# Planning steps 28 to 31 of the first pair with the rest, loading the weights in another order, and a subtraction moved to another engine

## The chip, the cores and the metric

The kernel runs on one core of a Trainium2 chip. The metric is the device time of one execution in microseconds (us), as the median of several runs. The engines are named as in the profile: PE (matmul; PEld is its weight load), DVE (vector), ACT (scalar), POOL (GpSimd) and SP, which here issues nearly all DMAs. Each engine works through its own queue in order. An instruction that waits for a semaphore holds up everything behind it on that engine.

## The reference

```python
B, H, S, Ns, D = (8, 8, 512, 32, 64)      # x: (B,H,S,D), state: (B,H,Ns,D)
scores = scale * np.matmul(x, state.transpose(0, 1, 3, 2))
a = softmax(scores);  xread = np.matmul(a, state)
scores2 = scale * np.matmul(state, x.transpose(0, 1, 3, 2))
a2 = softmax(scores2); sread = np.matmul(a2, x)
attn_out = np.concatenate([xread, sread], axis=2)
x = attn_out.transpose(0, 2, 1, 3).reshape(B * (S + Ns), H * D)   # 4352 x 512
h = x @ w_in                                # 512 x 2048
g = h * np.cos(h)
return g @ w_out                            # 2048 x 512
```

(`softmax` stands for the reference's maximum, subtraction, exponential and division.)

## The kernel before

**Tiles and steps.** A batch has 512 tokens. A tile is 128 of the 2,048 hidden columns by the 512 tokens of a batch, so a batch has 16 tiles (NF) and a pair of batches 32 (PERIOD). Step n of the program belongs to tile n. Since `xread` is a product with the small `state`, the kernel multiplies `state` with `w_in` ahead of time (`products`, kept in `sw_all`), and a tile is then one product of depth 256 with the attention weights `aT_all`: `hidden` (line 476). A tile's cosine gate follows on two engines in turn: `gate` (ACT, 547), `gate2` (DVE, 550), `gate3` (ACT, 553) and `gate4` (DVE, 567), which writes g into a slot of `g_all` and frees the tile's PSUM bank for the next tile but one. In the first pair two banks are used for single tiles; from the third batch on, tiles go in twos and by seven products of half size in place of eight (`seven_part`, `seven_sum`, `sw_sums` and `halves` make and use the sums).

**The output products.** g @ w_out is made for two batches together, as a 2 by 2 block product, again by seven block products in place of eight. Two of its blocks in the first pair are plain: `first_product` (weights a11, quad 5) and `second_product` (weights a12, quad 6), eight PE parts each (621). The others (p5, p3, p6 and so on, `Product`, line 750) have seven stages each, whose weights come from blocks kept in DRAM through a ring of four buffers (`fetch_block`). The operands of p5 are differences of rows of g, made by `outer_sum`, and differences of quarters of those, made on POOL by `Product.sums`. A "quad" is a piece of `g_all` of four slots of 512 elements; quads 5 to 8 hold the four quarters a11, a12, a21, a22 of w_out, others hold g, raw data and temporaries. Rows 0 to 3 of g (`quads_of[0, r]`) are tiles 0-7, 8-15, 16-23 and 24-31; row 2 lies in quads 10 and 9.

**Conversion.** The weights arrive as 64-bit floats. `fetch(i)` loads piece i raw into the quad `SLOTS[i]`, and `convert` makes 32-bit floats of it by two ACT instructions ("1", line 219, and "2", line 222, which goes to the scratch `aS_all`, named E0 to E3), two on DVE ("b", 225, and "c", 228; "c" is the last to read the raw data) and one on POOL ("d", 233). Pieces 4, 5, 7, 8, 10 and 11 are of w_in; 6 and 9 are a11, 12 and 13 are a12, 14 and 16 are a22, and 15 and 17 are a21. The sums of these quarters that p5 and the others need are made by `inner_weight` on POOL (671) and `sums_of` (1304), and are sent to DRAM by SP (`send_raw`, 659; `send_inner`, 674).

**The order.** Up to step FIRST - 1 = 27 the order on each engine comes from a list scheduler inside the program: `first_pair_tasks` lists tasks with an engine, a cost, what they read and write, and a due step (k in the calls of `at_step`); `link` turns a due step into a due time and hands it back along the dependences; `first_pair` then walks an estimated time, takes at each point the task that can start soonest on its engine, within NEAR, and among these the one with the smallest due time plus four times its delay, and issues it. From step 28 on `later_pair` and the loop below it issue in an order written out by hand: gates, `part`s of the attention, `stages(step)` of the products, `outer_at`, `sums_at`, `weights_at`, output stores (`store`, sent by SP at the start of the next step) and loads (`load_now`). The tile of a step is computed by PE two steps ahead of its gate in this part.

```python
CONV = range(4, N_LOADS)
CONV_DUE = (3, 3, 3.5, 6, 6, 7, 9, 9.5, 11, 12, 13, 14, 15, 16)
...
for step, t in enumerate(all_tiles[FIRST:], FIRST):
    ...
    later_pair(step, t, all_tiles[step + 2:step + 3])
```

Of the kernel before, what the change touches and what calls it, by code (L numbers as in the profile page):

```python
# [22 lines left out]
def kernel(  # L23
# [47 lines left out]
    quads_free = [7]  # L71
# [110 lines left out]
    def out_load(m, f):  # L182
# [11 lines left out]
    SLOTS = ((9, 9, 10, 10, 11) + (3, 2, 9, 10, 11) + (3, 9, 10, 11)  # L194
             + (9, 10, 11, 9))
# [48 lines left out]
    class Attention:  # L244
# [182 lines left out]

        def keep2(self):
            nc.tensor.transpose(out=at[1][:, 0:P],
                                in_=self.sr.rearrange("p j d -> p (j d)"),  # L430
                                identity=ident)
# [82 lines left out]
    def seven_part(t, k):  # L514
        (b11, b12, b21, b22), swS = weights_of(t)
        aT, aS = aT_of[t.b], aS_all[:, t.b % 2]
        h1, h2 = [h_pairs[t.at][:, i] for i in range(2)]
        for out_, w, r, start in (
                ((h2[:, LO], b11, aT[:, 0, LO], True),
                 (h2[:, HI], swS[:, 0], aS[:, 0], False)),  # L520
                ((h2[:, LO], swS[:, 1], aS[:, 1], False),
                 (h1[:, LO], b12, aT[:, 1, LO], False)),
                ((h2[:, LO], b21, aS[:, 2], False),
                 (h1[:, HI], swS[:, 2], aT[:, 1, HI], False)),
                ((h2[:, LO], b22, aS[:, 3], False),))[k]:
            nc.tensor.matmul(out=out_, lhsT=w, rhs=r, start=start, stop=True,  # L526
                             skip_group_check=True)
        if k == 0:
            nc.scalar.copy(h1[:, LO], h2[:, LO])
            nc.scalar.copy(sums_all[:, 0], h2[:, HI])  # L530

    def seven_sum(t, k):
# [5 lines left out]

    quads_of = defaultdict(list, {(0, 0): [0, 1], (0, 1): [2, 3],
                                  (0, 2): [10, 9], (0, 3): [5]})  # L540
# [54 lines left out]

    def store(b, half, src):

        def go(ch):
            ot = osb.tile([P, S], F32, name="ot")
            nc.vector.transpose(out=ot.rearrange("p (j i) -> p j i", i=32),  # L600
                                in_=src.t[:, ch].rearrange(
                                    "p (j i) -> p j i", i=32))
            rows = out[b * T:b * T + S, :].rearrange("(j t) d -> t j d", t=32)
            src.done()

            def send():
                for q in range(P // 32):
                    c0 = HD * half + P * ch + 32 * q
                    nc.sync.dma_start(
                        out=rows[:, :, c0:c0 + 32],  # L610
                        in_=ot[32 * q:32 * q + 32].rearrange(
                            "p (j i) -> p j i", i=32))
            stores_due.append(send)
        n = now[0] + 2 * (now[0] < PERIOD - 4)
        later.extend([(n + 1, lambda: go(0)), (n + 2, lambda: go(1))])
# [19 lines left out]
    def second_kept(pr, ch):  # L635
        if ch == 0:
            pr.o = Held()
        plus(pr.o, ch, acc[ch], pr.u)
        if ch == 1:
            store(2 * pr.n, 0, pr.o)  # L640
# [59 lines left out]
    class Product:  # L700
# [17 lines left out]
        def sums(self, k):  # L718
            lo, hi = self.quads()
            engine = nc.gpsimd  # L720
            if k == 1:
                self.q1 = quads_free.pop(0 if self.n else 1)
                self.t1 = quad(self.q1)[:, :, LO]
                self.t2 = quad(self.q1)[:, :, HI]
                sub(engine, self.t1, lo[:, :, HI], lo[:, :, LO])
            elif k == 2:
                sub(engine, self.t2, hi[:, :, HI], self.t1)
            elif k == 3:
                self.t3 = lo[:, :, HI]
                if not self.in_place:  # L730
                    self.q3 = quads_free.pop(0)
                    self.t3 = quad(self.q3)[:, :, LO]
                sub(engine, self.t3, hi[:, :, HI], lo[:, :, HI])
            else:
                sub(engine, self.t1, hi[:, :, LO], self.t2)

        def stage(self, k, copy):
            pr, b, c = self.pr, self.b, self.c
# [10 lines left out]
            for i in range(QT):  # L749
                nc.tensor.matmul(out=o, lhsT=ring[(self.first + k) % NB][:, i],  # L750
                                 rhs=g[:, i], start=(start and i == 0),
                                 stop=(i == QT - 1), skip_group_check=True)
            t5, u2 = sums_all[:, 1], sums_all[:, 2]
            if k == 1:
                copy(b[:, LO], c[:, LO])  # L755
                copy(t5, c[:, HI])
            elif k == 2:
                nc.vector.tensor_tensor(u2, c[:, LO], t5, op=ALU.add)
                self.sums(4)
            elif k == 3:  # L760
                copy(b[:, HI], u2)  # L761
            elif k == 4:
                nc.vector.tensor_tensor(c[:, HI], c[:, LO], t5, op=ALU.add)
                if not self.in_place:
                    quads_free.append(self.q3)
                if self.frees:
                    quads_free.append(quads_of[self.row][0])
            elif k == 5:
                self.out(0, b)
                if self.frees:  # L770
                    quads_free.extend(quads_of[self.row][1:])
            elif k == 6:
                self.out(1, c)
                quads_free.append(self.q1)
# [28 lines left out]
    products = []  # L803
# [260 lines left out]
    A11, A12, A21, A22, SQ = 5, 6, 7, 8, 11  # L1064
    temps = [quad(TEMPS), aS_all.rearrange("p n i s -> p (n i s)").rearrange(
        "p (t s) -> p t s", s=S)]
    for at_, freed in ((27, A22), (27, TEMPS), (28, SQ)):
        weights_at[at_].append(lambda freed=freed: quads_free.append(freed))
# [22 lines left out]
    FIRST = PERIOD - 4  # L1091
# [8 lines left out]
    def first_pair_tasks():  # L1100
# [124 lines left out]
        def attention_late(b, k):  # L1225
# [7 lines left out]
            for j in range(2):  # L1233
                add("pe", 1.05, lambda j=j: (part(b, "reads", j) if b > 1
                                   else a.reads(j)),
                    f"xT{j} {x}", "at0", k + 1 + j)
            for i in range(NK):
                add("dve", .3, lambda i=i: a.keep((i,)), "at0 i20 i21", "sr",
                    k + 2)
            if b < 2:  # L1240
                add("pe", .2, a.keep2, "sr", "at1", k + 3)
                add("act", .18, a.keep3, "at1", f"sT{b}", k + 3)

        def products(b, nt, k, c0=0, c1=WC):
# [3 lines left out]
            if nt == 0 and c1 - c0 == WC:  # L1248
# [3 lines left out]
                    for j in range(2)]  # L1252
            sw = [f"sw{nt % 2}{h}{j}" if half else
                  f"sw{nt % 2}0{j} sw{nt % 2}1{j}" for j in range(2)]
            add("pe", .55 if half else 1.05,
                lambda: attn[b].products(nt, SIDE, c0, c1), w + f" stT{b // 4}",
                " ".join(side), k)
            for j in range(2):
# [4 lines left out]
                        nt, SIDE, c0, c1,  # L1263
# [3 lines left out]
        def tile_(t, k):  # L1267
# [10 lines left out]
            add("dve", dve(512) - .02, lambda: gate4(t), f"h{h} q{h}", g)  # L1278
# [40 lines left out]
        def second(i, k):  # L1319
# [3 lines left out]
            if i == NH - 1:  # L1323
                for ch in range(2):
                    add("dve", .6, lambda ch=ch: second_kept(pr, ch),
                        "acc held0", "held1", k + 1)

        for b in (1, 2):
            attn[b] = Attention(b)
# [12 lines left out]
        for step, what in (  # L1342
# [7 lines left out]
                (5, lambda: attention(1, 6)),  # L1350
# [3 lines left out]
                (13, lambda: attention_late(1, 14)),  # L1354
# [4 lines left out]
                (16, lambda: inner(3, matrix(SQ), SQ, temps[1], E, 17)),  # L1359
                (17, lambda: sums_of(A22, SQ, A11, sub_, 18, "pool")),  # L1360
                (17, lambda: attention(2, 19)),
# [3 lines left out]
                                   names(TEMPS), 20)),  # L1365
                (20, lambda: sends(1, a12, 6, 22)),
                (21, lambda: inner(4, matrix(A22), A22, temps[1], E, 22)),
# [4 lines left out]
                (25, lambda: attention_late(2, 25)),  # L1372
                (24, lambda: [add("sp", .4, lambda n=n: fetch_block(n), "B3",
                                  f"ring{n}", 27) for n in range(NB - 1)])):
            at_step[step].append(what)
        for step, t in enumerate(all_tiles[0:FIRST]):
# [3 lines left out]
            if 4 <= step < 4 + NH:  # L1380
                first(step - 4, step - 1)
            if 13 <= step < 13 + 2 * NH and step % 2:
                second((step - 13) // 2, step)
        for i in range(2):
            o, x1, x2 = 0, 10, 0
            n = range(2 * i, 2 * i + 2)
            add("dve", dve(1024), lambda i=i: outer_sum(nc.vector, 0, 0, 2, 0,
                                                        0, i),
                names(10, *n) + " " + names(0, *n), names(0, *n), 27, True)
        return tasks  # L1390

    CONV = range(4, N_LOADS)
    CONV_DUE = (3, 3, 3.5, 6, 6, 7, 9, 9.5, 11, 12, 13, 14, 15, 16)
    PACE, NEAR, SEND = 3.6, .3, 2.5
# [37 lines left out]
    def first_pair():  # L1432
        now[0] = FIRST - 1
# [20 lines left out]
        while can:  # L1454
            best = None
            for e in free:
# [4 lines left out]
                for t in mine:  # L1461
                    at_ = max(free[e], ready[t])
                    if t.shares and pool_busy[0] <= at_ < pool_busy[1]:
# [4 lines left out]
                        key=lambda t: t.due + 4.0 * (starts[t] - soon))  # L1468
# [28 lines left out]
        for what in weights_at[FIRST - 1]:  # L1497
            what()
        for what in outer_at[FIRST - 1]:
            outer_sum(*what)  # L1500
        for pd, k in sums_at[FIRST - 1]:
            pd.sums(k)
        load_now(4)
# [52 lines left out]
    for step, t in enumerate(all_tiles[FIRST:], FIRST):  # L1556
        s, even = step % NF, step % 2 == 0
        if (s == 0 or step == FIRST) and t.b < B:
            steps = plan(t.b)
# [67 lines left out]
```

## Time and profile before

| what | value |
|---|---|
| median of 3 runs | 740.38 us (738.02 to 741.12) |
| profiled execution, its own time | 741.05 us |
| its span | 739.2 us |
| PE busy / DVE / POOL / ACT | 707.2 / 509.2 / 544.1 / 340.4 us |
| first tile's matmul | 22.24 us |
| tile 16, matmul and `gate4` | 99.26 and 103.56 us |
| tile 28, matmul | 143.00 us |
| first PE instruction of step 32 | 164.72 us |

The profile gives busy time by engine and stretch, groups of instructions by line with the idle time before them and what ended it, a chain of work followed back from the end, and the instructions in order of time. Times inside an execution are counted from the span's start. Lines L476, L621, L750 and L526 are PE's tiles, plain products, staged products and half-size tiles.

### The profile page before, as it was taken

To read this page: it belongs to the slowest core of one execution; us is meant where nothing else is said; L and a number is where in the kernel's file an instruction comes from. 1 tells how busy PE (TensorE), PEld (TensorE's weight loads), DVE (VectorE), ACT (ScalarE), POOL (GpSimd) and SP (SyncE) were. 2 spreads that over 40 slices of the span, in tenths; PEclk is the share of its full clock that TensorE was granted. 3 is DMA by queue.
4 is the path that set the end of the run, shared out by engine and by line. 5 is a ranking of instruction groups with operands and counts; after the bars stand their busy time and mean duration, and the time that the engine had idled before them with its cause. 6 is when DMAs were issued, how large, how long until landed. Compare 5 with 4: busy or idle time off the path is not lost.

```text
span 739.2 us, 10736 instructions
## 1 busy us (share of the span) xinstructions
PE 707.2 (96%) x3610; PEld 516.6 (70%) x3610; DVE 509.2 (69%) x716; ACT 340.4 (46%) x563; POOL 544.1 (74%) x528
## 2 busy tenths in 40 slices
PE   8899898699999999999999999999999999999997
PEld 3343333277778778777778788777688788888886
DVE  5989899876866668849756577768665467355550
ACT  5888867344463446344634464344634533211110
POOL 2467489587998997588998665879989665799600
PEclk9999999999999999999999999999999999999999
DMA  9984998846245954692238735752225465345661
GB/s 299 271 240 151 268 215 251 253 108 136 85 128 120 209 176 111 144 198 86 78 84 167 162 96 113 144 159 84 73 68 120 114 213 135 108 156 202 161 157 38
DMA packets 212471, 112.40 MB, mean 152 GB/s; under 512 B 158336, under 2 KB 175232, under 8 KB 212416
## 3 DMA queue, kind: packets, MB, share of 16 engines
q1 hardware_dynamic: 211328, 111.19, 57.4%
q8 instruction: 29, 0.48, 0.3%
q10 hardware_dynamic: 960, 0.39, 0.2%
q14 instruction: 26, 0.21, 0.1%
q0 software_dynamic: 128, 0.13, 0.1%
HBM read 88.08 MB, written 23.59 MB: 151 GB/s over the span
## 4 chain that ended last, share of the span: by engine, by line
PE 60%; POOL 21%; DVE 10%; issue 3%; ACT 3%; DMA 1%; SPq 0%; POOLq 0%; DVEq 0%; ACTq 0%
PE o L750 29%; POOL g_all L697 16%; PE h L526 13%; PE h L476 8%; POOL swS_all L509 3%; PE at L308 3%; PE at L851 2%; PE o L621 2%; PE at L413 2%; POOL sw_all L509 2%; DVE g_all L697 1%; DVE g_all L567 1%; DVE w_in L228 1%; DVE q_all L550 1%; PE o L851 1%
## 5 line engine op out<-in xcount | busy, mean ns | idle before, releaser
L697 POOL TENSOR_TENSOR g_all<-g_all 128x512 f32<-128x512 f32 x256 | 336.6, 1348 | 65.2 <-DVE g_all L697 48.7
L750 PE MATMUL o<-g_all 128*128 128x256 f32 x1456 | 344.1, 381 | 2.4 <-POOL g_all L697 2.4
L750 PEld LDWEIGHTS o<-g_all 128*128 128x128 f32 x1456 | 273.5, 190 | 49.7 <-issue 5.5
L550 DVE TENSOR_TENSOR q_all<-q_all,h 128x1024 f32<-128x1024 int32 (+1 forms) x88 | 85.1, 970 | 44.2 <-ACT q_all L547 43.9
L547 ACT ACTIVATE q_all<-h 128x1024 int32<-128x1024 f32 (+1 forms) x88 | 73.0, 834 | 86.3 <-PE h L526 35.1
L553 ACT ACTIVATE q_all<-q_all,halfpi 128x1024 f32<-128x1024 f32 (+1 forms) x88 | 84.0, 956 | 40.5 <-DVE q_all L550 40.2
L567 DVE TENSOR_TENSOR g_all<-h,q_all 128x1024 f32<-128x1024 f32 (+1 forms) x88 | 85.7, 974 | 19.8 <-ACT q_all L553 18.3
L535 DVE TENSOR_TENSOR h<-h,sums_all 128x256 f32<-128x256 f32 x96 | 41.2, 429 | 75.9 <-PE h L526 55.9
L476 PE MATMUL h<-aT_all,sw_all 128*128 128x512 f32 x128 | 63.6, 623 | 13.4 <-DVE g_all L567 12.5
L526 PE MATMUL h<-aT_all,sw_all 128*128 128x256 f32 x192 | 59.6, 392 | 3.8 <-DVE g_all L567 3.4
L526 PE MATMUL h<-aS_all,swS_all 128*128 128x256 f32 x192 | 60.2, 395 | 2.6 <-ACT sums_all L530 1.8
L526 PE MATMUL h<-aS_all,sw_all 128*128 128x256 f32 x192 | 58.0, 384 | 0.2
L697 DVE TENSOR_TENSOR g_all<-g_all 128x1024 f32<-128x1024 f32 x40 | 57.0, 1441 | 0.1
L476 PEld LDWEIGHTS h<-aT_all,sw_all 128*128 128x128 f32 x128 | 22.9, 191 | 45.9 <-DVE g_all L567 22.0
L526 PEld LDWEIGHTS h<-aS_all,swS_all 128*128 128x128 f32 x192 | 33.9, 189 | 27.0 <-issue 11.3
L755 ACT COPY o<-o 128x256 f32<-128x256 f32 x26 | 9.3, 357 | 85.4 <-PE o L750 85.4
L526 PEld LDWEIGHTS h<-aT_all,sw_all 128*128 128x128 f32 x192 | 34.5, 189 | 16.3 <-DVE g_all L567 12.2
L509 POOL TENSOR_TENSOR swS_all<-sw_all 128x128 f32<-128x128 f32 x48 | 22.8, 475 | 29.1 <-ACT sw_all L450 29.1
L761 ACT COPY o<-sums_all 128x256 f32<-128x256 f32 x26 | 9.8, 378 | 68.8 <-PE o L750 68.8
L526 PEld LDWEIGHTS h<-aS_all,sw_all 128*128 128x128 f32 x192 | 35.6, 190 | 8.4 <-DVE h L535 2.7
L233 POOL TENSOR_TENSOR w_in<-w_in,aS_all 128x1024 int32<-128x1024 int32 (+1 forms) x10 | 21.2, 2131 | 26.8 <-DVE w_in L228 24.9
L590 DVE SCALAR_TENSOR_TENSOR held<-o,held 128x512 f32<-128x512 f32 x40 | 27.2, 681 | 13.7 <-PE o L750 13.1
(115 smaller groups left out, 924.8 us busy)
## 6 DMA issues: line engine op xcount, KB each, us to landing
g_all<-blocks_kept SPq DMA_DIRECT2D x206, 256.0 KB, 2.8
blocks_kept<-g_all SPq DMA_DIRECT2D x48, 256.0 KB, 3.7
g_all<-in_moe_w_out_dram SPq DMA_DIRECT2D x8, 1024.0 KB, 5.7
out_dram<-ot SPq DMA_DIRECT2D x128, 64.0 KB, 2.0
g_all<-in_moe_w_in_dram SPq DMA_DIRECT2D x6, 1024.0 KB, 6.2
xT<-in_x_dram SPq DMA_DIRECT2D x96, 64.0 KB, 2.9
x_b<-in_x_dram SPq DMA_DIRECT2D x24, 256.0 KB, 4.7
x_b<-in_x_dram SPq DMA_DIRECT2D x16, 128.0 KB, 4.1
```

Of the source, the lines that this page charges most:

```text
L308: nc.tensor.matmul(out=(to or at)[j][Ns * k:Ns * k + Ns, n0:n1], lhsT=w[D * j:D * j + D, self.b, Ns * k:Ns * k + Ns], rhs=r(slice(D * j, D ...
L476: nc.tensor.matmul(out=t.hp, lhsT=t.lhs(i), rhs=t.rhs(i), start=(i == 0), stop=(i == t.kn - 1))
L509: nc.gpsimd.tensor_tensor(o, x1, x2, op=op)
L526: nc.tensor.matmul(out=out_, lhsT=w, rhs=r, start=start, stop=True, skip_group_check=True)
L535: nc.vector.tensor_tensor(o, h2[:, LO], sums_all[:, 0], op=ALU.add)
L547: nc.scalar.activation(t.q.bitcast(I32), t.hp, func=ACTF.Copy, bias=0.25)
L550: nc.vector.tensor_tensor(t.q, t.q.bitcast(I32), t.hp, op=ALU.subtract)
L553: nc.scalar.activation(t.q, t.q, func=ACTF.Sin, bias=halfpi, scale=-TWO_PI)
L567: nc.vector.tensor_tensor(g, t.hp, t.q, op=ALU.mult)
L590: nc.vector.scalar_tensor_tensor(out=out.t[:, ch], in0=bank, scalar=TWO_PI, in1=b.t[:, ch], op0=ALU.mult, op1=ALU.add)
L697: engine.tensor_tensor(o[:, i:i + n], x1[:, i:i + n], x2[:, i:i + n], op=ALU.subtract)
L750: nc.tensor.matmul(out=o, lhsT=ring[(self.first + k) % NB][:, i], rhs=g[:, i], start=(start and i == 0), stop=(i == QT - 1), skip_group_ch ...
```

## The change

The list scheduler takes tiles 0 to 31 (`FIRST = PERIOD`), and with them everything that the hand order did in steps 28 to 31: the second half of the first outer sum, five of the seven stages of p5 with their POOL sums and fetches, the loads of batch 3, the halves and weight sums of batch 2, the seven half-size products of tile 32, p3's first POOL sum and the two output stores. The conversion order puts a22 and a21 (14 to 17) ahead of a12 (12, 13), and the raw data go into quads 9, 10 and 6, no longer into 11. The second product's eight parts come at steps 16 to 27 (before 13 to 27, every other one), the first product's are due 1.5 steps later. The outer sum (2, 3, 2, 0) goes from POOL to DVE and into the planned part. Scaling `sread` by the inverse sums (`keep`, four DVE instructions of 32 rows) becomes eight ACT instructions (`keep_scaled`) for batches 1 and 2. The weight of a delay in the scheduler's choice goes from 4 to 8.

```diff
-    SLOTS = ((9, 9, 10, 10, 11) + (3, 2, 9, 10, 11) + (3, 9, 10, 11)
-             + (9, 10, 11, 9))
+    SLOTS = ((9, 9, 10, 10, 11) + (3, 2, 9, 10, 6) + (3, 9, 9, 10)
+             + (10, 6, 9, 10))
+        def keep_scaled(self, k):
+            rows = slice(Ns * k, Ns * k + Ns)
+            for j in range(2):
+                c0 = 2 * D * j + D * (k % 2)
+                nc.scalar.activation(self.sr[rows, j],
+                                     at[0][rows, c0:c0 + D], func=ACTF.Copy,
+                                     scale=self.i2[rows, j:j + 1])
-    FIRST = PERIOD - 4
+    FIRST = PERIOD
             for i in range(NK):
-                add("dve", .3, lambda i=i: a.keep((i,)), "at0 i20 i21", "sr",
-                    k + 2)
+                if b:
+                    add("act", .36, lambda i=i: a.keep_scaled(i),
+                        "at0 i20 i21", "sr", k + 2)
...
+        def outer(o, x1, x2, half, k, engine):
+            q, a_, b_ = [quads_of[0, r][half] for r in (o, x1, x2)]
+            for i in range(2):
+                n = range(2 * i, 2 * i + 2)
+                add(engine, dve(1024) if engine == "dve" else 2 * pool(512),
+                    lambda i=i: outer_sum(nc.vector if engine == "dve"
+                                          else nc.gpsimd, 0, o, x1, x2, half,
+                                          i), ...
+        def p5_tasks(k):
+            ...
+                add("pool", 4 * pool(512), lambda i=i: pd.sums(i), r, w,
+                    k - 3 + i)
...
+        t32, t34 = all_tiles[PERIOD], all_tiles[PERIOD + 2]
+                (26, lambda: outer(0, 2, 0, 0, 26, "dve")),
+                (27, lambda: outer(0, 2, 0, 1, 27, "dve")),
+                (28, lambda: tokens_of_next(30)),
+                (28, lambda: products(2, 0, 28)),
+                (28, lambda: p5_tasks(30.0)),
+                (29, lambda: weight_columns(t32, 30)),
...
+                (30, lambda: seven_tasks(t32, 30)),
+                (31, lambda: weight_columns(t34, 32)),
+                (32, lambda: outer(2, 3, 2, 0, 32, "dve")),
+                (32, lambda: p3_sums(32))):
             if 4 <= step < 4 + NH:
-                first(step - 4, step - 1)
-            if 13 <= step < 13 + 2 * NH and step % 2:
-                second((step - 13) // 2, step)
+                first(step - 4, step - -0.5)
+            for i in range(NH):
+                if SECOND_AT[i] == step:
+                    second(i, step)
-    CONV = range(4, N_LOADS)
-    CONV_DUE = (3, 3, 3.5, 6, 6, 7, 9, 9.5, 11, 12, 13, 14, 15, 16)
+    SECOND_AT = (16, 17, 19, 20, 22, 24, 26, 27)
+    CONV = (4, 5, 6, 7, 8, 9, 10, 11, 14, 15, 16, 17, 12, 13)
+    CONV_DUE = (3, 3, 3.5, 7.5, 6, 8.5, 9, 9.5, 10.5, 11, 12, 13.8, 14, 15)
-                        key=lambda t: t.due + 4.0 * (starts[t] - soon))
+                        key=lambda t: t.due + 8.0 * (starts[t] - soon))
```

The stores are made by a function `stored` that returns its four DMAs, so that the scheduler can place the DVE transposition and the sending apart; `Product.stage` is split into `multiply` and `follow` for the same reason. A few other due steps of the weights' sums and of the attention are moved by one to three steps.

## The prediction

> **What bounds the kernel.** I read the page first: PE is busy for 96% of the span, and the forty slices show where it is not, at the start, around slices 7 to 8 of the first pair, and at the end. Then I cut the time up to 200 us into stretches. The columns are PE, PEld, DVE, ACT and POOL busy, granted clock, DMA share and GB/s.
>
> ```profile
> 40.00:77.48 37.48, 32.62 (x133) 13.99 (x133) 34.15 (x39) 30.95 (x45) 25.74 (x12) 1.00 0.64 209
> 77.48:124.00 46.52, 46.28 (x197) 18.68 (x198) 42.35 (x62) 33.13 (x53) 33.12 (x21) 0.96 0.88 229
> 124.00:147.56 23.56, 15.88 (x77) 6.37 (x75) 20.35 (x28) 9.88 (x15) 15.29 (x12) 0.93 0.90 268
> 147.56:164.72 17.16, 17.16 (x75) 12.63 (x68) 12.12 (x18) 8.41 (x16) 13.97 (x17) 1.00 0.41 92
> 40.00:140.00 100.00, 90.23 (x385) 37.88 (x385) 91.75 (x120) 72.03 (x108) 71.64 (x42) 0.98 0.82 239
> 40.00:164.72 124.72, 111.94 (x472) 51.67 (x473) 108.97 (x144) 82.37 (x127) 88.11 (x60) 0.97 0.75 212
> 164.72:200.00 35.28, 34.73 (x189) 26.36 (x188) 28.49 (x36) 13.53 (x24) 30.93 (x31) 1.00 0.49 120
> ```
>
> Up to 140 us DVE is at 91.75%; PE has all its spare time here too. The bound changes hands: DVE in 40-77, PE in 77-124 (46.28 of 46.52), DVE again in 124-147, PE from 147.56 on. From step 32 (164.72) PE is at 98%, so a microsecond won before 164.72 reaches the end, and one won behind it doesn't show here. What stops PE before 165 us is one thing, the gate of an earlier tile on DVE; the columns are the total, how often, and the longest.
>
> ```profile
> PE h L476 <- DVE g_all L567: 10.8, 6, 4.5
> ```
>
> Two of these stalls are long. The instructions in order of time show them, with the wait in brackets:
>
> ```profile
> 77.48 2.61 PE L476 MATMUL h<-aT_all,sw_all 128*128 128x512 f32 x4 [3.82 <-DVE g_all L567]
> ...
> 136.54 1.98 PE L476 MATMUL h<-aT_all,sw_all 128*128 128x512 f32 x4
> 143.00 3.27 PE L476 MATMUL h<-aT_all,sw_all 128*128 128x512 f32 x4 [4.47 <-DVE g_all L567]
> ```
>
> A tile costs 1.72 us in the chain of waits elsewhere. After each long stall it costs more: 2.61 and then 2.79 for the next product, and 3.27 and then 1.36 in place of 1.02. That is 1.96 and 1.89 us. In both stretches of 5.5 us the granted clock is 0.69; after the stalls of 1.47 us and less it stays at 1.00. So PE's useful work in 40-164.72 is 111.94 - 3.85 = 108.1 us.
>
> Why tile 28 waits until 143.00 is on DVE:
>
> ```profile
> 135.37 2.04 DVE L697 TENSOR_TENSOR g_all<-g_all 128x1024 f32<-128x1024 f32 x1
> 137.34 0.87 DVE L423 TENSOR_TENSOR sr<-at,i_all 32x128 f32<-32x128 f32 x3
> 138.23 1.61 DVE L697 TENSOR_TENSOR g_all<-g_all 128x1024 f32<-128x1024 f32 x1
> 139.87 0.30 DVE L423 TENSOR_TENSOR sr<-at,i_all 32x128 f32<-32x128 f32 x1
> 140.18 0.69 DVE L590 SCALAR_TENSOR_TENSOR held<-o,held 128x512 f32<-128x512 f32 x1
> 140.79 1.27 DVE L550 TENSOR_TENSOR q_all<-q_all,h 128x512 f32<-128x512 int32 x2
> ```
>
> The outer sum and the scaling are queued ahead of the gates of tiles 26 and 27, and PE has nothing else: the eight second products were used up by 124 us.
>
> **The change part by part.** I count up to the first PE instruction of step 32, since both programs have the same work done there.
>
> DVE. Removed: 8 scalings of batches 1 and 2 (0.58 + 0.60 + 0.87 + 0.30 = 2.35 us in the rows of L423). Added: the outer sum (2, 3, 2, 0), two instructions of 128x1024; L697 on DVE took from 1.22 (148-149 us) to 2.04, on average 1.44, so 2.4 to 4.1, and I take 2 x 1.44 = 2.9. Gates, halves, transpositions and conversions stay in number. Sum: 108.97 - 2.35 + 2.9 = 109.5 us.
>
> ACT. 16 new instructions of 32x64 out of PSUM. The nearest rows are L434 (128x128 out of PSUM, 0.28) and L352 (128x2, 0.19): 3.0 to 4.5 us, nearer to L434, so 4. They lie in stretches where ACT is at 33.13 of 46.52 and 9.88 of 23.56. Without that cover a gate behind one waits 0.28 us.
>
> POOL. Removed: four instructions of 1.27 = 5.1 us at 161-171. In the whole kernel L750 waited 2.4 us for POOL, so this is worth 0 to 2.4; I take 0, because PE is full right behind it. POOL's inner sums (101.33 to 136.33 before) can begin sooner, since a21 and a22 no longer wait for a12.
>
> That last point can cost something. DVE's conversion at 72.08 took 3.27 us in place of 1.23; POOL's instruction ran from 71.58 to 74.26, and 74.26 + 1.1 is just its end. So a DVE instruction that comes behind a POOL one waits it out. POOL's share is 33.12 of 46.52 us in 77-124; an inner sum of 1.27 delays a collision by 0 to 1.27. Of the 14 conversions and two dozen other two-input instructions perhaps ten more meet one, at half of it: 6 us on DVE at worst, and 0 if as many collisions go from 101-136. I take 0, since the POOL instructions are moved and not added. The Trainium skill (SBUF — State Buffer, "Who interferes with whom") says that a DVE instruction with two SBUF inputs and a GpSimd one that reads SBUF lock each other out for the whole instruction, the first to issue winning; that speaks against bringing an outer sum to DVE next to p5's POOL sums. By the rule both new instructions would wait out a POOL one, and the sum would be the 4.1 above, 1.2 us more than mine.
>
> PE. No work is added. The second products go from steps 13-27 to 16-27 and the first ones 1.5 steps back, so 10 to 14 us of fillers leave 77-124, where PE is the bound, and lie in 124-147 and around 77, where it waits. The two clock losses (3.85 us) go if no stall of 3.8 us is left.
>
> SP. 48 block sends, the two stores (eight DMAs; 1.95 us for four at 158.35) and the loads of batch 3 are now issued in the planner's order. The transfers are used at 90% in 124-147. p5's fetches stand behind the stores; if a store waits for its transposition, a stage waits for its block: 0 to 2 us, taken as 0, since three blocks are fetched ahead.
>
> The sum. The same engine stays the bound, and the question is its share. If DVE keeps in the last 25 us the 91.75% that it has in 40-140, step 32 begins at 40 + 109.5 / 0.9175 = 159.3 and not at 164.72: 5.4 us. PE would be at 108.1 / 119.3 = 91% until then, about what it has in 40-140 (90.23), so it doesn't forbid this. The profiled execution would go from 741.05 to 735.7, the median of the runs (0.67 lower) from 740.38 to **735.0 us**.
>
> Bounds. The best 10 us slices of DVE have 96.5 to 97.4%; 96.5% throughout gives 40 + 113.5 = 153.5, a gain of 11.2 (729.2). With the whole stretch's share as it was, 108.97 / 124.72 = 87.4%, step 32 begins at 165.3: a loss of 0.6 (741.0).
>
> **The rivals.** *More than forecast* (0.10): PE's fillers and the tail both fall into place, 727 to 732. For it: PE and DVE alone need only 108 to 110 us of 124.72. Against it: they need each other, and DVE never held 96% for over 10 us at a time.
>
> *No difference* (0.17): the stalls move and DVE's share stays at 87.4%: 741. For it: the tail's DVE work (halves, transpositions, gates of four tiles) waits on PE and can't be drawn forward. The planner prices p5's sums at five us, while a sum is two POOL instructions of 1.27, so its order in the tail rests on wrong times.
>
> *Slower* (0.23): the raw quads become the wait. Before, pieces 12 to 17 went through quads 9, 10 and 11; now 14, 17 and 13 all follow piece 8 in quad 10, which tile 16's `gate4` must write next. The fetches, each right behind the last DVE "c" of its quad:
>
> ```profile
> 47.54 4.27 SPq L206 DMA_DIRECT2D g_all<-in_moe_w_out_dram  x2
> ...
> 71.50 0.37 SPq L206 DMA_DIRECT2D g_all<-in_moe_w_out_dram  x1
> ...
> 84.23 0.39 SPq L206 DMA_DIRECT2D g_all<-in_moe_w_out_dram  x1
> ```
>
> From a fetch to the end of its "c" pieces 12 to 17 took 23.9, 23.9, 19.5, 17.6, 19.9 and 12.6 us, mean 19.6. Piece 8's "c" ended at 47.48. Three turns at the mean end at 106.3; tile 16's `gate4` was at 103.56. Over (103.56 - 47.48) / 3 = 18.7 us a turn, tile 16 is later than before. At the mean it is 2.7 us late, PE has no second product yet (a12 is converted last) and pays a clock loss of 1.9: 740.38 + 4.6 = 745. Against it: the last piece needed 12.6 (8.4 of it for the DMA, by ACT's wait at 92.67), and three such turns end at 85.3; the long turns were work put off, not waiting for data. The collisions with POOL above would end in the same place, 740.38 - 5.4 + 6 = 741, or slower together with it.
>
> **How the numbers follow.** The forecast itself (732 to 736.7) has 0.50, more than forecast 0.10, no difference 0.17, slower 0.23. About 0.5% (3.7 us, 736.7 to 744.1) is what a measurement of this kernel can tell from no change. So faster 0.60, same 0.17, slower 0.23. The range reaches from the first bound with some of the POOL gain (728.5) to just over the slower case (746); cases of both signs hold much of the chance, and the forecast's own range is 732 to 736.7.
>
> **What would show it.** Right: step 32's first PE instruction at 157 to 162; stalls of PE behind L567 under 7 us in 40-165 and none over 3; L621 spread to 140 us; DVE over 90% until step 32; the rest from step 32 to the end unchanged within 1 us. Wrong: `gate4` of tile 16 later than 104 us behind an ACT or DMA wait; DVE conversions stretched over 2 us in numbers; L750 waiting for a block; or the time won before step 32 lost again behind it on POOL or DVE, which I price at nothing.

## The result and the profile after

The changed kernel takes 750.38 us (median of 4 runs, 749.98 to 751.37) against 740.75 us for the kernel before beside it; the ratio is 1.0139, with a 95% interval of 1.0110 to 1.0167. It is 10 us slower where 5 us faster was forecast. Its profiled execution has a span of 748.2 us, 9.0 more than before. Cut at two marks that both programs have, the first tile on PE and the first PE instruction of step 32, the stretches show where. First the kernel before, then the changed one (PE, PEld, DVE, ACT and POOL busy, granted clock, DMA share, GB/s):

```profile
22.24:164.72 142.48, 127.06 (x569) 58.87 (x570) 126.01 (x171) 98.18 (x149) 97.44 (x64) 0.98 0.77 217
...
164.72:739.20 574.48, 561.68 (x2968) 449.91 (x2966) 370.27 (x523) 230.90 (x397) 440.82 (x454) 1.00 0.52 130
```

```profile
33.95:173.65 139.70, 127.77 (x570) 59.43 (x570) 126.38 (x166) 98.54 (x163) 102.09 (x64) 0.98 0.73 206
...
173.65:748.20 574.55, 561.59 (x2968) 449.92 (x2966) 369.93 (x523) 231.81 (x398) 434.85 (x449) 1.00 0.53 130
```

The first tile comes at 33.95 and not at 22.24: 11.71 us lost. From there to step 32 the new order needs 139.70 in place of 142.48: 2.78 won. Behind step 32 nothing changes (0.07). Together that is the 9.0. So two things are to be explained: a stall ahead of the first tile, and a gain half as large as forecast.

The stall is on ACT. These are its instructions in order of time, before and after, around the first exponential (L348):

```profile
14.97 0.66 ACT L222 ACTIVATE aS_all<-g_all 128x512 int32<-128x512 uint32 x1
15.54 1.14 ACT L348 ACTIVATE aT_all<-aT_all 128x512 f32<-128x512 f32 x2
16.95 1.16 ACT L219 ACTIVATE w_in<-g_all 128x1024 f32<-128x1024 f32 x1 [0.28 <-DMA g_all<-in_moe_w_in_dram]
```

```profile
15.00 0.67 ACT L222 ACTIVATE aS_all<-g_all 128x512 int32<-128x512 uint32 x1
28.31 1.12 ACT L219 ACTIVATE g_all<-g_all 128x1024 f32<-128x1024 f32 x1 [12.64 <-DMA g_all<-in_moe_w_out_dram]
29.33 1.14 ACT L348 ACTIVATE aT_all<-aT_all 128x512 f32<-128x512 f32 x2
```

A conversion of a piece of w_out now stands ahead of the exponential of batch 0, and its data are not there. The exponential needs nothing of it, but ACT works in order. Behind the exponential the whole first attention waits: DVE stands still for 12.53 us until 29.98, and PE for 12.41 until its first tile. SP's queue says why the data are late:

```profile
9.15 13.87 SPq L143 DMA_DIRECT2D held<-in_state_dram  x8
23.07 0.43 SPq L206 DMA_DIRECT2D g_all<-in_moe_w_out_dram  x1
```

The eight loads of the state hold SP until 23.0 us, as they did before (9.29 to 22.9). The fetch goes out at 23.07 and lands 5.2 us later. The planner, though, starts with `"sp": 10.0`, as it did before: it believes that SP can issue at 10 us. Piece 9's raw data now go into quad 6, which nobody has used, so nothing in the plan holds its fetch back; by the planner's own costs it arrives at about 15 us, and ACT is given the conversion there. Before, the same piece went into quad 11 and had to wait for piece 4 to leave it (piece 4 goes there in both programs).

The lines that answer to those of before follow. They are cut at the same times from the span's start, while the changed program is 9 to 12 us behind the one before at the same tile, so they show where PE waits and not tile against tile. The third of the waits is that of before, from the first tile to step 32:

```profile
20.00:40.00 20.00, 7.59 (x26) 3.32 (x19) 9.34 (x18) 8.68 (x16) 2.82 (x2) 0.66 0.48 155
...
77.48:124.00 46.52, 38.93 (x169) 15.36 (x168) 42.85 (x51) 32.93 (x52) 37.40 (x21) 0.96 0.91 245
124.00:147.56 23.56, 21.55 (x81) 8.29 (x79) 22.77 (x31) 15.41 (x26) 20.64 (x14) 1.00 0.95 308
```

```profile
PE h L484 <- DVE aT_all L389: 12.4, 1, 12.4
PE h L484 <- DVE g_all L580: 10.2, 9, 2.2
PE h L476 <- DVE g_all L567: 12.5, 8, 4.5
```

PE is busy for 7.59 of the 20 us from 20 to 40 (16.62 before), at a clock of 0.66 (L484 and L580 are the old L476 and L567). In 124-147, where it had 15.88 us of work before, it has 21.55, and no stall behind a gate is over 2.2 us. But the total of these waits is 10.2 us where it was 12.5, a fall of 2.3, which is most of the 2.78 won: PE now waits in 77-124, where it is busy for 38.93 us in place of 46.28.

### The profile page after: what moved, and what is told of

Its sections match the earlier page's. It is cut to its first block, busy times and chain, and to the rows that moved or that the text cites. A ratio compares the mean times of both kernels' runs of the same rounds, so it can differ in the third digit from the quotient of the medians.

```text
span 748.2 us, 10735 instructions
## 1 busy us (share of the span) xinstructions
PE 707.6 (95%) x3610; PEld 517.0 (69%) x3610; DVE 508.3 (68%) x710; ACT 343.4 (46%) x579; POOL 542.7 (73%) x524
## 4 chain that ended last, share of the span: by engine, by line
PE 55%; POOL 21%; DVE 9%; DMA 6%; issue 3%; ACT 3%; SPq 2%; DVEq 0%; POOLq 0%
PE o L767 29%; POOL g_all L710 16%; PE h L539 12%; PE h L484 6%; DMA g_all<-in_moe_w_out_dram 4%; POOL swS_all L517 3%; PE at L308 2%; PE at L872 2%; POOL sw_all L517 2%; PE at L413 2%; DVE g_all L228 2%; DMA g_all<-blocks_kept 1%; DVE g_all L710 1%; DVE g_all L580 1%; PE o L872 1%
## 5 line engine op out<-in xcount | busy, mean ns | idle before, releaser
L710 POOL TENSOR_TENSOR g_all<-g_all 128x512 f32<-128x512 f32 x252 | 333.0, 1350 | 66.8 <-DVE g_all L710 43.2
L580 DVE TENSOR_TENSOR g_all<-h,q_all 128x1024 f32<-128x1024 f32 (+1 forms) x88 | 85.6, 974 | 20.0 <-ACT q_all L566 18.7
L484 PE MATMUL h<-aT_all,sw_all 128*128 128x512 f32 x128 | 63.9, 629 | 22.8 <-DVE aT_all L389 12.4
L484 PEld LDWEIGHTS h<-aT_all,sw_all 128*128 128x128 f32 x128 | 23.5, 196 | 56.8 <-DVE g_all L580 20.7
L710 DVE TENSOR_TENSOR g_all<-g_all 128x1024 f32<-128x1024 f32 x42 | 61.2, 1475 | 0.1
L233 POOL TENSOR_TENSOR w_in<-w_in,aS_all 128x1024 int32<-128x1024 int32 (+1 forms) x10 | 23.2, 2339 | 39.8 <-DVE w_in L228 36.6
```

The costliest lines, as they stand in the source:

```text
L233: nc.gpsimd.tensor_tensor(bits, bits, e, op=ALU.add)
L484: nc.tensor.matmul(out=t.hp, lhsT=t.lhs(i), rhs=t.rhs(i), start=(i == 0), stop=(i == t.kn - 1))
L580: nc.vector.tensor_tensor(g, t.hp, t.q, op=ALU.mult)
L710: engine.tensor_tensor(o[:, i:i + n], x1[:, i:i + n], x2[:, i:i + n], op=ALU.subtract)
```

## The experiments

Ratios are to the kernel before, run on the same chip, with 95% intervals. "Mended" is the third kernel below, the changed one with the planner's entry set right. Each edit makes the scheduler lay out the whole first pair anew, and each trace is one execution; so a difference of 0.001 between two of these kernels can't be put down to the edited line alone.

**Raw data in quad 11.** The changed kernel with the two users of quad 6 sent to quad 11.

```diff
-    SLOTS = ((9, 9, 10, 10, 11) + (3, 2, 9, 10, 6) + (3, 9, 9, 10)
-             + (10, 6, 9, 10))
+    SLOTS = ((9, 9, 10, 10, 11) + (3, 2, 9, 10, 11) + (3, 9, 9, 10)
+             + (10, 11, 9, 10))
```

> The changed kernel, but the raw data of pieces 9 and 15 go into quad 11 as before and not into quad 6, so that no fetch can be planned before piece 4 has left quad 11. Theory (the whole loss is the start: ACT's first instruction of piece 9 stands ahead of the first exponential and waits 12.64 us for its data): first tile at 22.0 to 22.8, no ACT wait over 2 us before it, step 32 at 159 to 163, time 734 to 740. Rival (the rest of the new plan looked 2.8 us quicker only because the data came in during the stall): first tile at 22.0 to 22.8 too, but step 32 at 164 to 168 and time 740 to 744.

Measured: 738.92 us against 740.74, ratio 0.9968 (0.9953 to 0.9982); first tile at 21.98, step 32 at 163.38. The stall is gone and with it all of the loss. The median lies where the theory put it, while step 32 in the one profiled execution falls between the two accounts.

**The quad alone, in the kernel before.** One number changed.

```diff
-    SLOTS = ((9, 9, 10, 10, 11) + (3, 2, 9, 10, 11) + (3, 9, 10, 11)
+    SLOTS = ((9, 9, 10, 10, 11) + (3, 2, 9, 10, 6) + (3, 9, 10, 11)
```

> The kernel before with one number changed: the raw data of piece 9 go into quad 6. Theory (that free quad is what lets the planner put piece 9's first ACT instruction ahead of the first exponential): first tile at 33 to 35, step 32 at 173 to 177, time 748 to 753. Rival (the stall comes from the new due steps or the weight of 8 and not from the quad): first tile at 22 to 23 and 738 to 742.

Measured: 753.15 us, ratio 1.0153 (1.0122 to 1.0184), first tile at 33.86, step 32 at 176.63: the theory. ACT's rows are the changed kernel's:

```profile
28.22 1.12 ACT L219 ACTIVATE g_all<-g_all 128x1024 f32<-128x1024 f32 x1 [12.33 <-DMA g_all<-in_moe_w_out_dram]
29.24 1.14 ACT L348 ACTIVATE aT_all<-aT_all 128x512 f32<-128x512 f32 x2
```

None of the rest of the change is needed for the stall. The loss of this one number (1.5%) is that of the whole change and a little more.

**The planner's entry (mended).** Quads as in the change.

```diff
-                "sp": 10.0}
+                "sp": 22.5}
```

> The changed kernel, quads as changed, but the planner is told that SP's queue is free at 22.5 us, as the trace has it (22.7), and not at 10.0. Theory (the wrong entry is the time at which the planner thinks SP can issue): piece 9's ACT instruction goes behind the first exponential, first tile at 22.0 to 22.8, time 734 to 740, within 1.5 us of the run with quad 11. Rival (the plan is slower in itself): first tile at 22.0 to 22.8, step 32 at 164 to 168, 740 to 744. If the quad itself is at fault and not the planner's entry, the first tile stays behind 30 us and the time over 746.

Measured: 738.61 us, ratio 0.9964 (0.9948 to 0.9980), first tile at 22.16, step 32 at 160.71 (its profiled execution, 736.64, is the quickest of the 12). The free quad does no harm once the planner knows when SP is free. What the rest of the change is worth is thus 0.36% of 740.74, 2.7 us (1.5 to 3.9), not the 5.4 forecast. Its stretches, and those of the kernel before, tell where the rest stays. Mended first, then before, both from 40 us to step 32:

```profile
40.00:70.00 30.00, 29.46 (x121) 12.37 (x119) 28.48 (x37) 26.36 (x37) 21.08 (x11) 1.00 0.58 193
70.00:95.00 25.00, 17.99 (x92) 7.06 (x92) 23.00 (x28) 19.55 (x30) 18.68 (x9) 0.93 0.89 237
95.00:160.71 65.71, 63.27 (x258) 31.01 (x258) 53.51 (x75) 38.78 (x75) 54.31 (x42) 1.00 0.79 218
```

```profile
40.00:70.00 30.00, 28.96 (x105) 12.58 (x106) 26.91 (x32) 24.26 (x33) 21.07 (x10) 1.00 0.64 213
70.00:95.00 25.00, 21.18 (x105) 9.35 (x104) 21.90 (x31) 21.29 (x32) 9.78 (x4) 0.93 0.85 216
95.00:164.72 69.72, 61.80 (x264) 29.75 (x263) 60.16 (x83) 36.82 (x64) 57.26 (x46) 0.98 0.76 209
```

From 95 us on the mended kernel has PE at 96% (before 89%), but in 70-95 at 72% (before 85%). The last first product ends at 67.8, and the first second product starts at 95.25, since a12 is converted last; in between PE has only tiles and pieces of the attention, and the tiles wait for their gates:

```profile
77.54 5.60 PE L484 MATMUL h<-aT_all,sw_all 128*128 128x512 f32 x8 [3.59 <-DVE g_all L580]
```

This is the stall that the kernel before had at 77.48 (3.82 us), with its clock loss: two tiles in 5.60 us, where others that nothing holds up take 3.60 to 3.70. The stalls of 124-147 are gone (no wait for a gate there is over 0.82 us), but in 70-95 PE is idle for 7.0 us where it was for 3.8.

**The outer sum on POOL again** (`outer(2, 3, 2, 0, 32, "pool")` in the mended kernel).

> The mended kernel (planner told that SP is free at 22.5) with the outer sum (2, 3, 2, 0) planned on POOL again, at the same place. Theory (the prediction's terms: DVE loses 2.9 us of work, PE is full there and POOL has room): ratio to the kernel before within 0.003 of the mended one's 0.9964. Rival (DVE is the bound up to step 32, so its 2.9 us come back): 0.991 to 0.994. Other rival (POOL's 5.1 us delay p5's and p3's sums or the weight columns): over 0.9995.

Measured: 0.9973 (0.9963 to 0.9983). The first account holds: on which engine this sum runs makes no difference that can be measured. But it says less than it seems to. In the mended kernel DVE makes the sum at 160.81, in 2.35 us, just behind the first PE instruction of step 32 (160.71), where PE is full. So the run doesn't test what this sum costs DVE ahead of step 32.

**The scaling on DVE again** (`if b:` in the mended kernel replaced, so that all batches use `keep`).

> The mended kernel with the scaling of batches 1 and 2 on DVE again (8 instructions of 0.29 us on DVE in place of 16 on ACT, whose eight took 2.04 to 2.06). Theory (every microsecond of DVE work before step 32 counts at 1 / 0.92): 2.35 / 0.92 = 2.6 us slower than the mended kernel, ratio 0.9985 to 1.001. Rival (DVE isn't what sets the pace in these places, as the stall of 3.59 us at 77 and full PE later suggest): within 0.0015 of 0.9964.

Measured: 0.9974 (0.9960 to 0.9987). The value lies in the rival's band; the interval's end touches the theory's. 2.35 us of DVE work cost 0.7 us at the middle of the estimates; with some 1 us either way on both ratios, nothing and 2 us can't be told apart, and 2.6 is hardly possible.

**The fillers' due steps as before.**

```diff
-                first(step - 4, step - -0.5)
+                first(step - 4, step - 1)
-    SECOND_AT = (16, 17, 19, 20, 22, 24, 26, 27)
+    SECOND_AT = (13, 15, 17, 19, 21, 23, 25, 27)
```

> The mended kernel with the due steps of the two plain products as before (first product 1.5 steps earlier, second product at steps 13, 15 to 27). Theory (late fillers are what fills PE in 124 to 147): stalls behind L580 in 120 to 147 of 3 us or more come back and the ratio to before is 0.9985 to 1.002. Rival (the converted a12 comes late anyway and sets when the second products can go, so the due steps do little): within 0.0015 of 0.9964, and stalls as in the mended kernel.

Measured: 0.9997 (0.9986 to 1.0008). The ratio is the theory's, the mechanism isn't. No stall of 3 us comes back in 120-147. PE is busy for 15.96 of the 25 us in 70-95, and there it even stops for a filler:

```profile
97.79 3.49 PE L636 MATMUL o<-g_all 128*128 128x512 f32 x4 [3.92 <-POOL g_all L233]
```

A second product that is due early stands at the head of PE's queue and waits for the conversion of a12, which now comes last. The later due steps fit the new conversion order; they are no gain by themselves.

**POOL's sums at their true price** (`2 * pool(512)` for `4 * pool(512)` in p5's and p3's tasks of the mended kernel).

> The mended kernel with p5's and p3's POOL sums priced in the planner at two instructions (2.5 us), as the trace has them, and not at four (5.0). Theory (the planner's wrong price puts p5's stages later in PE's queue than they need be, with PE waiting for tiles meanwhile): p5's first stage 2 to 4 us earlier, ratio 0.992 to 0.995. Rival (PE has no other wait in the tail than a tile's gate, and p5's order doesn't matter): within 0.0015 of 0.9964.

Measured: 0.9975 (0.9965 to 0.9985), first stage of p5 at 141.12 (139.47 in the mended kernel). The theory falls: the wrong price costs nothing that can be seen. The traces say one thing more. In this plan the outer sum lies ahead of step 32 again (149.58 and 155.70), and from the first tile to step 32 DVE is busy for 126.60 of 140.60 us; with the raw data in quad 11 the sum lies behind (163.50), and DVE is busy for 122.98 of 141.40 us. So 3.6 us more of DVE work did not lengthen the stretch.

**The conversion order as before** (with the raw quads of before; this kernel, the next two and that with the scaling on DVE also let `multiply` read t1 and t2 only where they are set, which changes no instruction).

```diff
-    CONV = (4, 5, 6, 7, 8, 9, 10, 11, 14, 15, 16, 17, 12, 13)
+    CONV = range(4, N_LOADS)
```

> The mended kernel with the conversion order (a12 before a22 and a21) and the raw quads as before, everything else as changed. Theory (with a12 converted last PE has no second product between 68 and 95 us and idles 7 of 25 us there, while it is full from 95 on): first second product before 85 us, PE busy over 20.5 us in 70 to 95, ratio to the kernel before 0.990 to 0.994. Rival (a22 and a21 first is what lets p5 start early; with them late POOL's sums end 10 us later and p5 waits): first stage of p5 behind 145 us and ratio 0.9985 to 1.003.

Measured: 0.9976 (0.9963 to 0.9988). The theory's first half came true: the first second product is at 77.65, and PE is busy for 21.75 us in 70-95. The gain did not come, and nor did the rival's late p5 (138.99). The stalls went back to where they had been:

```profile
123.19 5.14 PE L484 MATMUL h<-aT_all,sw_all 128*128 128x512 f32 x8 [2.87 <-DVE g_all L580]
...
145.98 5.40 PE L484 MATMUL h<-aT_all,sw_all 128*128 128x512 f32 x8 [2.16 <-DVE g_all L580]
```

**Conversion order and second products as before** (the run above with `SECOND_AT` of before).

> As the run before, and the second product due at steps 13, 15 to 27 again. Theory: the second products fill 70 to 95 still better, ratio 0.988 to 0.994. Rival (they then run out before 124, and the stalls of the kernel before come back at 124 to 147): a stall of 3 us or more behind 120 us and ratio 0.996 to 1.000.

Measured: 0.9982 (0.9970 to 0.9994), a stall of 3.07 us at 124.61. The rival holds.

**Half of a12 first.** The mended kernel with an order in between the two; the raw quads are new with it.

```diff
-    SLOTS = ((9, 9, 10, 10, 11) + (3, 2, 9, 10, 6) + (3, 9, 9, 10)
-             + (10, 6, 9, 10))
+    SLOTS = ((9, 9, 10, 10, 11) + (3, 2, 9, 10, 11) + (3, 9, 10, 11)
+             + (9, 11, 10, 9))
-    CONV = (4, 5, 6, 7, 8, 9, 10, 11, 14, 15, 16, 17, 12, 13)
+    CONV = (4, 5, 6, 7, 8, 9, 10, 11, 12, 14, 15, 16, 17, 13)
```

> The mended kernel with only a12's first half (piece 12) converted ahead of a22 and a21, raw data in quads 9, 10 and 11. Theory: four second products can go before 95 and a22 and a21 are hardly later, ratio 0.990 to 0.994. Rival (DVE sets the pace of the tiles before 95, so a PE filler moved there leaves a gap later): within 0.0015 of 0.9964.

Measured: 736.94 us against 741.16, ratio 0.9942 (0.9925 to 0.9959). It is the quickest of all, 0.58% faster than the kernel before. The interval overlaps the mended kernel's, so that it beats that one as well is likely and not shown. Three second products, not the four of the theory, now lie ahead of 95 us and five behind, PE is busy for 20.56 us in 70-95, and no wait behind a gate is over 1.9 us:

```profile
70.00:95.00 25.00, 20.56 (x121) 8.79 (x120) 21.47 (x30) 20.38 (x29) 12.85 (x6) 1.00 0.72 211
```

## Why the prediction was wrong

**The sign.** The prediction asked what the raw quads would do and looked at quad 10, reused three times late; it did not look at quad 6, used for the first time early. It took each piece as fetched right behind the last "c" of its quad, and so didn't see that a quad with no earlier user has its fetch planned at once. In the text the failed step is the start of the sum, "40 + 109.5 / 0.9175": it begins at 40 us, and what lies ahead of that was taken as the same in both programs. The trace of before showed that SP is held from 9.29 for 13.60 us, and the code has `"sp": 10.0`; side by side they could have told it. The runs put the whole loss there: the one number in the kernel before gives 1.0153, and either mending takes it away.

**The rival "slower".** It named raw quads and a time of 745, but another mechanism, and that one didn't happen: in the mended kernel tile 16's `gate4` is at 103.63 (before 103.56), three us behind the end of the last "c" (100.17), and waits for ACT's sine and not for a quad.

**The size.** The second term that failed is the share in "109.5 / 0.9175". The work was right: from the first tile to step 32 DVE is busy for 126.38 us in the changed kernel and for 126.01 before, 0.4 more where 0.5 was forecast. But its share went from 88.4% to 90.5% only, where the forecast needs 92.3% (126.5 us of work in 142.48 - 5.4), and 2.78 us were won there and not 5.4. Nor does the amount of DVE's work set the pace: 2.35 us of it put back cost 0.7 by the middle values, and in one plan 3.6 us more did not lengthen the stretch. The bound of 96.5% rests on a misreading too: DVE's best 10 us before are 60-70, with 10.00, and it is busy for 28.89 of the 30 us from 110 to 140, so it did hold 96% for over 10 us.

What the traces fit is that PE needs a filler at the moment when a gate is behind other things in DVE's queue. The plan has 16 such fillers, the parts of the two plain products, and each order spends them somewhere: before, they ended at 124; in the mended kernel, they ran out at 68 and came again at 95; with the old conversion order and the new plan, they end at 120 again. The prediction counted the 10 to 14 us of fillers as gained in 124-147 and as free to leave 77-124, because PE was full there. It was full because of them. This account is read from the traces; no run changed the fillers alone and showed a gain clear of the mended kernel's.

**What held.** What is won or lost ahead of step 32 reaches the end unchanged (behind it 574.55 us in the changed and 574.19 in the mended kernel, 574.48 before). POOL's relief is worth nothing behind step 32, where POOL is busy for 434.85 us in place of 440.82. The two instructions of the outer sum took 2.19 and 1.38 us in the changed kernel, 3.57 in all where 2.9 was taken. By the Trainium skill's rule on the shared port (SBUF — State Buffer, "Who interferes with whom") both would have waited out a POOL instruction, 4.1 in all: the longer one ran while POOL was busy (160.58 to 166.70), and in the mended kernel, with POOL idle, the two took 2.35. In the time of the whole kernel nothing of it can be seen. ACT's scaling took 2.04 to 2.06 us for a batch, as the 4 us for two had it, and was hidden: PE's one wait for it in the mended kernel is 0.24 us.

## What to carry to other kernels

A planner inside a program is only as good as the times that it starts from: when a change makes a resource free from the beginning, look at what then can be planned first, and set it against the time at which the trace shows the queue free. An instruction that waits for its data costs little where nothing of worth is queued behind it, and everything ahead of a serial chain's first step. Where one engine is full, ask which of its work could have gone elsewhere before pricing that work as free to move.

## What was not expected of the hardware

SP's queue stays on eight small loads of the state (32 KB each) for 13.06 to 14.04 us in all 12 traces, while seven larger loads (0.5 and 1 MB) are on their way; the loads of weights take 0.37 to 0.61 us of SP each. In the kernel before, 6.0 us of this are waits that by the profile end with the landing of an earlier load of weights. Why the queue doesn't take the small loads sooner was not tried.

A POOL instruction holds up more than the two-input instructions of DVE: the one-input shift (L225, 128x1024) took 0.69 us alone, and 2.51 at 65.81 in the mended kernel, with POOL converting from 62.17 to 67.75.

PE's clock falls after shorter stalls than the kernel before showed, and not after every one. There it fell after 3.82 and 4.47 us and stayed after 1.47. The changed kernel has two stalls of nearly the same length:

```profile
92.89 1.98 PE L484 MATMUL h<-aT_all,sw_all 128*128 128x512 f32 x4 [2.20 <-DVE g_all L580]
...
98.03 3.12 PE L484 MATMUL h<-aT_all,sw_all 128*128 128x512 f32 x4 [2.13 <-DVE g_all L580]
```

After the first the granted clock stays at 1.00 up to 98.00; after the second it is 0.63 over 4.6 us. In the last experiment a stall of 1.86 us at 123.98 was followed by two tiles in 5.40 us (3.60 to 3.70 at full speed) and a granted clock of 0.66 over 5.0 us, while with the fillers' due steps as before one of 3.11 at 78.30 left it at 1.00. After the same stall of 3.59 us at 77 the next two tiles took 5.60, 6.23 and 6.77 us in three of the kernels (mended, quad 11, POOL's sums at their price). The Trainium skill (TensorE: Matmul & The Clock Gate, "What's actually happening") ties the fall to an idle window of about 3.4 us; stalls of 1.86 and 2.13 are shorter than that, so by these rows the length of one stall does not decide alone.
